# Issuing 48 weight loads from GpSimd's software queue instead of SyncE

## The chip, the core and the metric

The kernel runs on one core of a Trainium2 chip. The core has a matrix engine (TensorE, PE in the rows), VectorE (DVE), ScalarE (ACT), GpSimd (POOL) and SyncE (SP). SyncE computes nothing here: it issues transfers, which 16 DMA engines then carry out. The metric is the device time of one execution in microseconds, the median of several runs.

## What is computed

Two layers follow each other. The first is attention through a packed query, and a three-way max of matrix products; the second sends each of 4608 tokens to one of eight experts.

```python
p_packed = sm_attn(p, k, v)
out = sm_attn(q, p_packed, p_packed)          # 8 batches, 8 heads, 576 tokens, head size 64
h = np.maximum(np.maximum(x @ w1, x @ w2), x @ w3)     # 512 -> 768
x = (h @ w_out)                                        # 768 -> 512
logits = x @ w_gate
e_idx = np.argmax(logits, axis=1)
...
h = np.maximum(x[mask] @ w1[e], 0.0)          # the token's expert, 512 -> 1024 -> 512
ye = h @ w2[e]
out[mask] = gate_w[mask, None] * eom[mask, e, None] * ye
```

## The kernel before

**Stages.** The first stage takes the eight batches one after the other: attention, then the products `mm1` (L1023, its operand `G` made at L996), then rows of the first layer's output, `mm2` (L1061), which end in `yrow` in device memory. The second stage goes over blocks of 128 tokens that share an expert: `hidden` (L1307, or L1317 and L1319) and `outer` (L1365), with the expert's weights in one of two buffers, `wbuf`.

**Numbers in two halves.** Products are in 16 bits, with each operand split into a high and a low half. A split is two steps: `scaled` (L197 on ScalarE, L204 on GpSimd, L206 or L208 on VectorE) makes the high half, and `less` (L215 or L217) the low half. Which engine takes a split is open where several are allowed.

**The preparation.** The experts' weights must be split too. As soon as the first 18 of 36 row tiles are known, the kernel counts which experts are used most (`ranking`, ending in `xe`, L410), and splits the weights of the first three experts while attention goes on. `expert_of` reads an expert's number from `xe` into a register (L529). `prep` does one of 48 pieces: a load of 128 x 512 floats (256 KB) into one of four buffers `pl` (L546), the high half (`scaled`) and the low half (`less`) into one of three buffers `po`, and a store of 256 KB to the scratch `wscr` (L553). The slot pools are `rb` (four `pl`) and `rd` (three `po`); a load may not go out before the `less` that read its buffer last has ended, and a split may not begin before the store of its `po` buffer has landed. Weights of other experts are prepared in the second stage (L1384, L1399), which the change doesn't touch.

**What sets the order.** The order of every engine's instructions is written down by a planner, `Flow`. Each step has a cost per engine that may take it, a rank and a list of steps to wait for; the planner always takes the step that can start first by its own count of time, on the engine where it ends first, and the recorded order of each engine is fixed by that. Where the planner sees TensorE pause for longer than a set limit, it puts in small products on constants (`fill`, L253), whose results nobody uses. So a changed cost of one step can move everything planned after it, on all engines. Engines run their instructions strictly in order, and SyncE issues its transfers strictly in order. The program is planned in two goes; the preparation lies in the first of them (`F.run()`, L1235).

Of the kernel before, what the change touches and what calls it, by code (L numbers as in the profile page):

```python
# [18 lines left out]
SP = mybir.EngineType.SP  # L19
# [5 lines left out]
E = 8  # L25
# [25 lines left out]
class Flow:  # L51
# [18 lines left out]
    def add(self, cost, fn, after=(), rank=0, take=(), give=(), move=0.0, behind=None):  # L70

        x = types.SimpleNamespace(cost=cost, fn=fn, rank=rank, take=take, give=give, move=move, n=self.count, end=None,
                                  ready={}, by=None, wait=0, then=[], next=[])
        self.count += 1
        for y in after:
            if y is None:
                continue
            if y.end is None:
                y.then.append(x)
                x.wait += 1  # L80
            else:
                x.ready[y.by] = max(x.ready.get(y.by, 0.0), y.end)
        if behind is not None and behind.end is None:
            behind.next.append(x)
            x.wait += 1
        if not x.wait:
            self.todo.append(x)
        return x
# [70 lines left out]
def body(ctx: ExitStack, tc, q, k, v, p, w1, w2, w3, wo, wg, wog, mw1, mw2, out):  # L159
    nc = tc.nc  # L160
    w1, w2, w3, wo = (x.bitcast(I32) for x in (w1, w2, w3, wo))
    act, dve, pool, pe, sp = nc.scalar, nc.vector, nc.gpsimd, nc.tensor, nc.sync
# [19 lines left out]
    xe = const.tile([1, E], I32, name="xe")  # L182
# [7 lines left out]
    engines = dict(act=act, dve=dve, pool=pool)  # L190
    F = Flow(dict(m=3, s=2, v=1, ra=2, rt=2, rc=2, mt=1, rb=4, rd=3, w=2, wx=3, kst=1, qst=1, v16=1, pT=1, PT=1, x32=4,
                  A16=2, pp16=2, plain=1, gp=4, t0=2, t1=2, hT0=1, hT1=1, row=2))
    add = F.add
# [5 lines left out]
    def scaled(e, o, i, scale=1.0):  # L199

        if e == "act":
            act_copy(o, i, scale)
        elif e == "pool":
            pool.tensor_scalar(out=o, in0=i, scalar1=scale, scalar2=1.0, op0=ALU.mult, op1=ALU.mult)  # L204
        elif isinstance(scale, float) and scale == 1.0:
            dve.tensor_copy(out=o, in_=i)  # L206
        else:
            dve.tensor_scalar(out=o, in0=i, scalar1=scale, scalar2=None, op0=ALU.mult)  # L208

    def less(e, o, i, hi, scale=1.0):  # L210

        if e == "pool" or isinstance(scale, float) and scale == 1.0:
            if not (isinstance(scale, float) and scale == 1.0):
                scaled(e, i, i, scale)
            engines[e].tensor_tensor(out=o, in0=i, in1=hi, op=ALU.subtract)  # L215
        else:
            dve.scalar_tensor_tensor(out=o, in0=i, scalar=scale, in1=hi, op0=ALU.mult, op1=ALU.subtract)  # L217

    def costs(n, **kw):

        c = dict(act=0.09 + n * 0.834e-3, dve=0.07 + n * 1.042e-3, pool=n * 2.175e-3, both=0.02 + n * 3.28e-3, quick=0.02 + n * 1.11e-3,
                 fast=0.07 + n * 0.521e-3)
        return {dict(fast="dve", both="pool", quick="pool").get(e, e): c[e] * m for e, m in kw.items()}
# [12 lines left out]
    def placed(slot, pool, shape, dt, name):  # L236
        return Lazy(lambda tag: pool.tile(shape, dt, tag=tag, name=name, bufs=1), slot)
# [38 lines left out]
    step, rank, of = [[]], [0], {}  # L276
# [138 lines left out]
    with ExitStack() as ph1:  # L415
# [108 lines left out]
        pld, pstart, stored = [], [], {}  # L524

        def expert_of(r):

            def f(e):
                of[r] = nc.values_load(xe[0:1, r:r + 1], engines=[SP], min_val=0, max_val=E - 1)  # L529
            pstart[:] = [add(dict(sp=0.5), f, after=pstart, rank=-600)]  # L530

        def prep(n, rank=1000):
            e, u = divmod(n, 16)
            t = placed("rb", rb, [128, 512], F32, "pl")
            o = placed("rd", rd, [128, 2, 512], F16, "po")
            if u < 8:
                kt, hf = divmod(u, 2)
                src = lambda: mw1[bass.ds(of[e], 1), kt * 128:(kt + 1) * 128, hf * 512:(hf + 1) * 512].rearrange("a r f -> (a r) f")
                sc = 128.0
                dst = wscr[e, :, kt * 2048:(kt + 1) * 2048].rearrange("r (l f) -> r l f", l=2)[:, :, hf * 512:(hf + 1) * 512]  # L540
            else:
                ft = u - 8
                src = lambda: mw2[bass.ds(of[e], 1), ft * 128:(ft + 1) * 128, :].rearrange("a r f -> (a r) f")
                sc = 256.0
                dst = wscr[e, :, 8192 + ft * 1024:8192 + (ft + 1) * 1024].rearrange("r (l f) -> r l f", l=2)
            ld = add(dict(sp=0.5), lambda e: sp.dma_start(out=t()[:], in_=src()), rank=rank, take=(t,), move=0.73, after=pstart,  # L546
                     behind=pld[-1] if pld else None)
            pld.append(ld)
            h = add(costs(512, act=1, fast=1, quick=1), lambda e: scaled(e, o()[:, 0], t()[:], sc), after=[ld], rank=rank, take=(o,))
            l = add(costs(512, both=1, dve=1), lambda e: less(e, o()[:, 1], t()[:], o()[:, 0], sc), after=[h], rank=rank,  # L550
                    give=(t,))
            stored.setdefault(e, []).append(
                add(dict(sp=0.5), lambda e: sp.dma_start(out=dst, in_=o()[:]), after=[l], rank=rank - 1, give=(o,), move=0.73))  # L553
# [638 lines left out]
        for r in range(NP1):  # L1192
            expert_of(r)
        p0, p1 = plan_r[3] + T_["p0"], plan_r[B - 1]
        for n in range(NU):
            prep(n, p0 + (p1 - p0) * n * T_["prep"] / NU + V("pr", n // 8))
# [457 lines left out]
```

## Time and profile before

| | |
|---|---|
| median of 3 runs | 1003.0 us (998.7 to 1004.31) |
| the profiled execution | 998.91 us, of which the profile's span is 997.2 us |
| TensorE busy | 910.6 us, 91% of the span |
| VectorE, ScalarE, GpSimd busy | 683.1, 434.9, 382.5 us |
| mean granted clock of TensorE | 0.971 of full speed |
| loads and stores of the preparation | 48 and 48, of 256 KB each |

The span begins at 0 and stretches are given in us from there. An engine's busy time doesn't count the time in which it waits; the idle time before an instruction is put down to what ended it. Instructions that SyncE spends on issuing transfers are not in its busy time, but stand in the trace with start and length.

### The profile page before, as it was taken

What the parts mean: (1) busy time and instruction counts of PE and PEld (TensorE: products, weight loads), DVE (VectorE), ACT (ScalarE), POOL (GpSimd) and SP (SyncE); (2) the same over time, 40 slices, a digit from 0 to 9 for tenths busy, and PEclk for the clock granted to TensorE, in tenths of its full rate; (3) what the DMA queues carried; (4) which work ended last, traced back from release to release, by engine and by line L of the source; (5) the groups of instructions that cost most, each with busy time, mean ns of one, the idle gap of its engine ahead of it and who ended that gap; (6) DMA issues with size and microseconds to landing.
All of it is one profiled execution on the core that took longest, in us unless ns stands there. A gap on an engine that the chain in (4) does not pass through costs nothing. (4 is left out here: it accounts for less than half of the span.)

```text
span 997.2 us, 24407 instructions
## 1 busy us (share of the span) xinstructions
PE 910.6 (91%) x9124; PEld 672.0 (67%) x9124; DVE 683.1 (69%) x1642; ACT 434.9 (44%) x898; POOL 382.5 (38%) x494
## 2 busy tenths in 40 slices
PE   8779988969899987878799998999999999999995
PEld 6547665757676765656577786776776766767663
DVE  3998687547749479588884569588786555555551
ACT  4534544446647354243333213364564433434431
POOL 0523363647766566277533323123222221211101
PEclk9989889989999998999999999999999999999999
DMA  9965478485865769979704177523322892334930
GB/s 269 307 198 140 108 203 207 105 207 118 181 170 108 206 199 245 263 218 282 213 1 167 48 206 259 134 66 98 66 76 86 259 237 65 87 76 149 319 50 29
DMA packets 219324, 160.23 MB, mean 161 GB/s; under 512 B 155903, under 2 KB 195839, under 8 KB 216128
## 3 DMA queue, kind: packets, MB, share of 16 engines
q1 hardware_dynamic: 213280, 139.17, 52.4%
q0 software_dynamic: 5920, 19.44, 6.3%
q8 instruction: 73, 1.20, 0.5%
q14 instruction: 51, 0.42, 0.1%
HBM read 240.33 MB, written 52.99 MB: 294 GB/s over the span
## 5 line engine op out<-in xcount | busy, mean ns | idle before, releaser
L1023 PEld LDWEIGHTS <-G 128*128 128x128 f16 x1728 | 172.5, 100 | 80.8 <-issue 18.3
L1023 PE MATMUL psm<-A,G 128*128 128x288 f16 x1152 | 166.5, 295 | 25.7 <-DVE G L217 21.0
L1365 PE MATMUL pso<-wbuf,h 128*128 128x512 f16 x816 | 181.8, 379 | 1.1 <-ACTq L1620 1.1
L1061 PE MATMUL pss<-wo,hT 128*128 128x264 f16 x1296 | 152.2, 281 | 5.4 <-DVE T L959 3.8
L1365 PEld LDWEIGHTS <-h 128*128 128x128 f16 x888 | 85.3, 98 | 97.7 <-issue 1.9
L1061 PEld LDWEIGHTS <-hT 128*128 128x128 f16 x1296 | 128.5, 100 | 27.8 <-issue 6.8
L1375 POOL DMA_INDIRECT out<-o,sidx x33 | 39.9, 1208 | 259.6 <-ACT o L1370 242.6
L1317 PE MATMUL psh<-xT,wbuf 128*128 128x256 f16 x736 | 110.4, 273 | 0.0
L215 POOL TENSOR_TENSOR hT<-t,hT 128x288 f16<-128x288 f32 x84 | 66.7, 795 | 107.4 <-ACT hT L197 67.8
L1023 PE MATMUL pss<-A,G 128*128 128x288 f16 x576 | 89.4, 293 | 0.7 <-ACT e L806 0.7
L1307 PEld LDWEIGHTS <-wbuf 128*128 128x128 f16 x1344 | 77.0, 98 | 3.9 <-DMA wbuf<-wscr 1.0
L1317 PEld LDWEIGHTS <-wbuf 128*128 128x128 f16 x736 | 65.3, 98 | 9.6
L1319 PE MATMUL psh<-xT,wbuf 128*128 128x128 f16 x736 | 71.0, 219 | 0.0
L1032 DVE SCALAR_TENSOR_TENSOR t<-psm,t 128x288 f32<-128x288 f32 x96 | 43.4, 452 | 34.0 <-PE psm L1023 26.1
L197 ACT ACTIVATE t<-psm 128x288 f32<-128x288 f32 x96 | 38.8, 405 | 61.4 <-PE psm L1023 59.3
L1282 ACT ACTIVATE xs<-g,brs 128x512 f16<-128x512 f32 x37 | 26.8, 724 | 78.0 <-DVE brs L1278 76.1
L1319 PEld LDWEIGHTS <-wbuf 128*128 128x128 f16 x736 | 56.6, 98 | 4.1
L217 DVE SCALAR_TENSOR_TENSOR G<-psm,G 128x384 f16<-128x384 f32 x96 | 49.8, 546 | 11.0 <-ACT G L197 10.4
L197 ACT ACTIVATE G<-psm 128x384 f16<-128x384 f32 x96 | 43.1, 487 | 31.4 <-PE psm L996 20.9
L1326 DVE TENSOR_TENSOR hs<-psh,hs 128x512 f32<-128x512 f32 x46 | 31.8, 691 | 35.0 <-ACT hs L197 33.9
L1307 PE MATMUL psh<-xT,wbuf 128*128 128x128 f16 x960 | 55.2, 219 | 0.0
L996 PE MATMUL psm<-wst,pp 128*32 128x384 f16 x672 | 37.4, 335 | 18.7 <-DVE G L217 14.3
(295 smaller groups left out, 1531.9 us busy)
## 6 DMA issues: line engine op xcount, KB each, us to landing
wbuf<-wscr SPq DMA_DIRECT2D x148, 1024.0 KB
pt<-in_moe_w SPq DMA_DIRECT2D x40, 512.0 KB
wscr<-po SPq DMA_DIRECT2D x40, 512.0 KB
pl<-in_moe_w SPq DMA_DIRECT2D x48, 256.0 KB
wscr<-po SPq DMA_DIRECT2D x48, 256.0 KB
ld<-in_k SPq DMA_DIRECT2D x14, 512.0 KB
ld<-in_q SPq DMA_DIRECT2D x14, 512.0 KB
ld<-in_v SPq DMA_DIRECT2D x12, 512.0 KB
```

What stands on the lines that cost most here:

```text
L197: act.activation(out=o, in_=i, func=AF.Copy, scale=scale)
L215: engines[e].tensor_tensor(out=o, in0=i, in1=hi, op=ALU.subtract)
L217: dve.scalar_tensor_tensor(out=o, in0=i, scalar=scale, in1=hi, op0=ALU.mult, op1=ALU.subtract)
L996: pe.matmul(o, lhsT=a.stat(h, l), rhs=wst[:, ft, :, h, :], start=(l == 0), stop=(l == 1), tile_position=(0, hh * 32))
L1023: pe.matmul(ps()[:, 0:288], lhsT=a.G[ft]()[:, g, lg, w * 128:(w + 1) * 128], rhs=a.A16()[:, g, la, c * 288:(c + 1) * 288], start=(n == 0), ...
L1032: e0 = add(costs(288, dve=1), lambda e, src=src, o=o: dve.scalar_tensor_tensor(out=o()[:], in0=src(), scalar=sc, in1=t0()[:], op0=ALU.mult ...
L1061: pe.matmul(view()[:, nh, 0:OG0], lhsT=hT()[:, ft, lh, c0:c0 + 128], rhs=wo16()[:, ft, lw, nh, :], start=(i == 0 and ft == 0), stop=(i == ...
L1307: pe.matmul(ps[:, f4 * 128:(f4 + 1) * 128], lhsT=w1v[:, kt, lw, cols], rhs=xT[:, lx, kt, :], start=(n + kt == 0), stop=(n == 2 and kt == 3))
L1317: pe.matmul(o.rearrange("r (l t) -> r l t", l=2), lhsT=w1v[:, kt, 0, cols], rhs=xT[:, :, kt, :], start=(kt == 0), stop=False)
L1319: pe.matmul(o[:, 0:128], lhsT=w1v[:, kt, 1, cols], rhs=xT[:, 0, kt, :], start=False, stop=(kt == 3))
L1365: pe.matmul(po, lhsT=h2[:, lh, ft, :], rhs=w2v[:, ft, lw, :], start=(n == 0), stop=(n == 23))
L1375: pool.indirect_dma_start(out=out, out_offset=bass.IndirectOffsetOnAxis(ap=idx, axis=0), in_=o[:], in_offset=None, bounds_check=NTOK - 1, ...
```

## The change

Two costs and two engines are exchanged: the three register reads and the 48 loads of `prep` go to GpSimd, the load with a planned cost of 1.0 instead of 0.5. What is loaded, into which buffers and after which steps stays the same. The stores stay on SyncE.

```diff
@@ -526,8 +526,8 @@
         def expert_of(r):
 
             def f(e):
-                of[r] = nc.values_load(xe[0:1, r:r + 1], engines=[SP], min_val=0, max_val=E - 1)
-            pstart[:] = [add(dict(sp=0.5), f, after=pstart, rank=-600)]
+                of[r] = nc.values_load(xe[0:1, r:r + 1], engines=[mybir.EngineType.Pool], min_val=0, max_val=E - 1)
+            pstart[:] = [add(dict(pool=0.5), f, after=pstart, rank=-600)]
 
         def prep(n, rank=1000):
             e, u = divmod(n, 16)
@@ -543,7 +543,7 @@
...
-            ld = add(dict(sp=0.5), lambda e: sp.dma_start(out=t()[:], in_=src()), rank=rank, take=(t,), move=0.73, after=pstart,
+            ld = add(dict(pool=1.0), lambda e: pool.dma_start(out=t()[:], in_=src()), rank=rank, take=(t,), move=0.73, after=pstart,
                      behind=pld[-1] if pld else None)
```

On GpSimd, this is what stood where the preparation begins (`hT` is the low half of an `mm1` result, `pl` a loaded buffer, `po` a split one):

```order
 L215 TENSOR_TENSOR hT<-t_5203,hT 128x288
-L215 TENSOR_TENSOR hT<-t_5238,hT 128x288
-L215 TENSOR_TENSOR hT<-t_5301,hT 128x288
-L204 TENSOR_SCALAR po<-pl 128x512
-L215 TENSOR_TENSOR hT<-t_5333,hT 128x288
-L204 TENSOR_SCALAR pl<-pl 128x512
-L215 TENSOR_TENSOR po<-pl,po 128x512
-L215 TENSOR_TENSOR hT<-t_5384,hT 128x288
-L903 COPY FC<-bt 64x1
-L903 COPY FC<-bt 128x1 x4
```

And this is what stands some rows behind that place now, after the three register reads and the first four loads (the number tells one buffer's use from the next):

```order
L204 TENSOR_SCALAR pl_5306<-pl_5306 128x512
L215 TENSOR_TENSOR po_5363<-pl_5306,po_5363 128x512
L204 TENSOR_SCALAR po_5433<-pl_5338 128x512
L546 ISA
L546 DMA pl_5447<-in_moe2_w1 128x512
L546 ISA
L546 DMA pl_5455<-in_moe2_w1 128x512
L546 ISA
L546 DMA pl_5480<-in_moe2_w1 128x512
L204 TENSOR_SCALAR pl_5350<-pl_5350 128x512
L215 TENSOR_TENSOR po_5487<-pl_5350,po_5487 128x512
L204 TENSOR_SCALAR po_5530<-pl_5447 128x512
```

The loads now stand between GpSimd's splits, so that each split behind a load waits until that load can go out, and four low halves `hT` of `mm1` have left this place.

On VectorE, at the same place of the program, the piece of the difference right behind `xe` shows where they went (`t` is the input of an `hT` half):

```order
 L410 TENSOR_SCALAR xe<-fcum 1x8
+L215 TENSOR_TENSOR hT<-t_5238,hT 128x288
 L1032 SCALAR_TENSOR_TENSOR t_5276<-psm,t_5276 128x288
-L1032 SCALAR_TENSOR_TENSOR t_5301<-pss,t_5276 128x288
-L1032 SCALAR_TENSOR_TENSOR t_5320<-psm,t_5320 128x288
...
+L215 TENSOR_TENSOR hT<-t_5329,hT 128x288
+L1032 SCALAR_TENSOR_TENSOR t_5348<-psm,t_5348 128x288
+L1032 SCALAR_TENSOR_TENSOR t_5374<-pss,t_5348 128x288
+L217 SCALAR_TENSOR_TENSOR po<-pl,po 128x512
```

VectorE takes those halves now. Over the whole program the planner's counts move as follows. GpSimd loses 12 high halves `po` (31 to 19), 6 low halves `hT` (84 to 78), 4 pairs of steps on `v` (43 to 39), one pair on `vt`, 2 low halves `tm` (13 to 11) and one step on `T`; it gains the 48 loads, 2 small copies to `LG`, one step each on `e` and `ph`, and one low half `A`. VectorE gains 6 high halves `po`, 6 low halves `hT`, 4 low halves on `v` and one on `vt`, 2 low halves `tm`, one step on `T` and a cast to `A`; it loses 4 casts to `hT`, one low half `A` and two steps on `ph`. ScalarE gains 6 high halves `po` and 4 casts to `hT`. On TensorE the fill products rise from 226 to 281 (L253); all else is the same work in another order.

## Rows read from the trace of the kernel before

**Rows 1.** The page's busy times and slices of the span.

```profile
PE 910.6 (91%) x9124; PEld 672.0 (67%) x9124; DVE 683.1 (69%) x1642; ACT 434.9 (44%) x898; POOL 382.5 (38%) x494
PE   8779988969899987878799998999999999999995
DMA  9965478485865769979704177523322892334930
```

**Rows 2.** Stretches: busy us and instructions per engine, PE clock, DMA share, GB/s.

```profile
353.40:494.90 141.50, 116.06 (x1200) 87.93 (x1198) 110.62 (x201) 60.59 (x125) 91.93 (x121) 0.95 0.89 245
500.00:550.00 50.00, 48.78 (x505) 37.51 (x503) 31.62 (x83) 18.97 (x44) 17.75 (x27) 1.00 0.25 97
700.00:750.00 50.00, 50.00 (x543) 36.24 (x541) 40.78 (x93) 29.64 (x50) 14.04 (x10) 1.00 0.34 76
```

**Rows 3.** Waits of PE from 353.4 to 494.9 (total us, times, longest).

```profile
PE psm L1023 <- DVE G L217: 6.9, 5, 1.7
PE psm L996 <- DVE G L217: 6.1, 3, 5.1
PE pss L1061 <- DVE T L959: 3.8, 1, 3.8
```

**Rows 4.** SyncE's own waits at L546 in the same stretch, the three largest.

```profile
SPq L546 <- DVE t L1032: 12.5, 7, 2.6
SPq L546 <- DVE po L217: 10.4, 9, 2.6
SPq L546 <- POOL po L215: 4.6, 3, 3.1
```

**Rows 5.** The loads on SyncE: ns min/median/max, first and last start.

```profile
L546 SPq DMA_DIRECT2D pl<-in_moe_w x48: 332/344/1769, 353.5 to 486.1; - x48
```

**Rows 6.** Transfers that GpSimd issues, in the second stage (same columns).

```profile
L1265 POOL DMA_INDIRECT g<-yrow,gidx x37: 996/1042/1602, 572.4 to 933.6; - x37
L1375 POOL DMA_INDIRECT out<-o,gidx x4: 1028/1440/2479, 612.7 to 651.1; - x4
```

**Rows 7.** GpSimd's groups from 353.4 to 494.9: count, busy us, mean ns, idle before.

```profile
L204 POOL TENSOR_SCALAR po<-pl 128x512 f16<-128x512 f32 x31 | 21.1, 680 | 31.3 <-DMA wscr<-po 24.8 <-DMA pl<-in_moe_w 5.0 <-issue 1.3
L215 POOL TENSOR_TENSOR hT<-t,hT 128x288 f16<-128x288 f32 x20 | 17.4, 870 | 7.1 <-DVE hT L206 3.9 <-ACT hT L197 3.2
L215 POOL TENSOR_TENSOR v<-ld,v 128x256 f16<-128x256 f32 x8 | 6.8, 844 | 0.7
L215 POOL TENSOR_TENSOR tm<-ld,tm 128x1024 f16<-128x1024 f32 x2 | 4.7, 2369 | 0.0
L204 POOL TENSOR_SCALAR ld<-ld 128x256 f32<-128x256 f32 x8 | 4.1, 513 | 0.0
L215 POOL TENSOR_TENSOR A<-U,A 128x576 f16<-128x576 f32 x1 | 1.8, 1793 | 0.0
```

**Rows 8.** VectorE's groups in the same stretch.

```profile
L217 DVE SCALAR_TENSOR_TENSOR po<-pl,po 128x512 f16<-128x512 f32 x37 | 35.7, 968 | 15.6 <-POOL po L204 11.5 <-ACT po L197 3.8
L206 DVE CAST hT<-t 128x288 f16<-128x288 f32 x9 | 3.7, 414 | 0.3
L215 DVE TENSOR_TENSOR hT<-t,hT 128x288 f16<-128x288 f32 x5 | 3.0, 601 | 0.2
L215 DVE TENSOR_TENSOR tm<-ld,tm 128x1024 f16<-128x1024 f32 x2 | 2.9, 1446 | 0.0
L208 DVE TENSOR_SCALAR po<-pl 128x512 f16<-128x512 f32 x1 | 0.4, 427 | 1.0 <-DMA wscr<-po 1.0
```

**Rows 9.** The same low half over the whole trace, min/median/max; one on `v`.

```profile
L217 DVE SCALAR_TENSOR_TENSOR po<-pl,po x37: 674/721/2614, 356.9 to 493.0; 128x512 f16<-128x512 f32 x37
L217 DVE SCALAR_TENSOR_TENSOR v<-ld,v x5: 410/425/542, 189.4 to 326.1; 128x256 f16<-128x256 f32 x5
```

**Rows 10.** SyncE in order of time from 494: start us, us, what it issues.

```profile
493.76 0.89 SPq L553 DMA_DIRECT2D wscr<-po  x2
526.08 12.51 SPq L1080 DMA_DIRECT2D yrow<-row  x4
539.65 2.10 SPq L1260 DMA_DIRECT2D wbuf<-wscr  x4
```

**Rows 11.** The fill products around the stretch, min/median/max.

```profile
L253 PE MATMUL psv<-ones x24: 216/219/288, 385.0 to 508.7; 128*128 128x128 f16 x24
```

## Prediction

> **What bounds the kernel now.** I read the page's busy times first: TensorE is busy for 91% of the span, so only a stage in which it is not full can give or take much [rows 1]. The slices show where that is: in the last two fifths TensorE is at 9 nearly throughout, in the first half it swings between 7 and 9. Then I cut out the stretch in which the preparation runs, from the first load's issue (353.4) to its last store (494.9). There TensorE is busy for 116.1 of 141.5 us, idle for 25.4; just behind it, from 500 to 550, it is busy for 48.8 of 50, and in the second stage for all of 50 [rows 2]. So the change is worth what it does to those 25.4 us.
>
> What TensorE waits for in that stretch is mostly VectorE: 13.0 us for the low halves of `G`, which give its PSUM banks back, and 3.8 for a transpose of scores [rows 3]. VectorE is busy for 110.6 us of 141.5 (78%), GpSimd for 91.9 (65%), ScalarE for 60.6 [rows 2]. The DMA engines are in use for 0.89 of it.
>
> How late the preparation itself may be: its last store is issued at 494, the first reader, the load of `wbuf`, at 539.7 [rows 10]. That is 45 us of room, so the 48 loads don't set the end by being late. They set it by what they hold up on the engine that issues them, and by what the planner moves away from that engine.
>
> **What comes off SyncE.** 48 issues of 0.344 us [rows 5] are 16.5 us. The queue also stood still before loads: the three rows shown are 27.5 us, and four further ones of 0.7, 0.6, 0.3 and 0.2 make it 29.3 [rows 4]. These are waits for a buffer `pl` to be free again (the `less` of an earlier piece), or for an earlier transfer. Behind them stood stores, transposes and loads of attention. What is gained is bounded by what TensorE waits for: its largest waits name VectorE and none names a transfer [rows 3]. I take 0 for the gain, with 9 us as its far end (the second rival).
>
> **What comes onto GpSimd.** The trace has no plain load issued by GpSimd. From below it is bounded by SyncE's issue, 0.344 us [rows 5], from above by the slowest of its scatters in this program, 2.479, with 1.440 as that group's median [rows 6]. The nearest row is the gather: also 128 rows of about 2 KB, also issued by GpSimd, 1.042 us in the median [rows 6]. I take that: 48 x 1.042 = 50.0 us. The ends are 48 x 0.344 = 16.5 and 48 x 1.440 = 69.1. The three register reads are left at nothing: right behind them stand the first four loads, whose data the next split waits for anyway.
>
> **What the planner takes off GpSimd.** By the counts in the section on the change and the means of [rows 7]: 12 high halves `po` at 0.680 (8.2), 6 `hT` at 0.870 (5.2), 4 pairs on `v` at 0.513 + 0.844 (5.4), 2 `tm` at 2.369 (4.7); for the pair on `vt` and the step on `T` I take 3 together, the size of the larger rows here. That is 26.5. It adds one `A` at 1.793, and for two `LG`, one `e` and one `ph` I take another 3.5, so 5.3 come back. Net, 21.2 us less.
>
> GpSimd's busy time in the stretch becomes 91.9 + 50.0 - 21.2 = 120.7 us. The waits for a free `pl` come with the loads: a load on GpSimd that has to wait for VectorE's `less` holds up the split behind it, and the `hT` and attention halves behind that. Taking all 29.3 us over gives 150.0 us in a stretch of 141.5: **8.5 us too much**. This counts no wait for stores, of which GpSimd now has 24.8 us [rows 7]; I take these as the cover in which loads can go out. If that cover is gone, up to 24.8 more would be due, which is the upper bound of this term; if the loads cost 0.344, the sum is 33.5 us lower and nothing is due; if 1.440, it is 19.1 higher, which by the sum below is 1030.6.
>
> **What comes onto VectorE.** 6 `po` at 0.427, 6 `hT` at 0.601, 2 `tm` at 1.446 [rows 8], 4 `v` at 0.425 [rows 9], and about 1 each for the steps on `vt` and `T`: 2.6 + 3.6 + 2.9 + 1.7 + 2 = 12.8. Off it go 4 casts at 0.414 (1.7) and about 2.5 for `ph` and `A` together with the cast gained: 8.6 us net, 110.6 to 119.2. One thing works against it. The low half `po` took 0.968 us in the mean here [rows 8], but 0.674 at its shortest [rows 9]: over 37 of them that is 10.9 us of stretching beside other work. GpSimd's work other than loads falls from 91.9 to 70.7 us; if the stretching falls in proportion, 0.23 x 10.9 = 2.5 us are given back, and VectorE ends at about 117, 6 us more than before. The Trainium skill, SBUF — State Buffer, "Who interferes with whom", says that a VectorE instruction with two SBUF inputs contends with a GpSimd instruction that reads SBUF, and not with one that only writes it; by that, a load in place of a split would do VectorE no harm, and 6 us is the figure, where without it the sum would be the full 8.6. Since TensorE waits for VectorE by name in this stretch [rows 3], 6 us there is worth at most 6 us. It lies beside GpSimd's 8.5 us, not behind it: both stretch the same 141.5 us. I take the larger, 8.5.
>
> **The fill.** 55 more fill products at 0.219 us [rows 11] are 12.0 us at most if TensorE would otherwise have worked, and nothing where it waits anyway. The planner put them where it saw pauses; I take 0, and the upper end keeps them.
>
> **The sum.** 998.9 us, the profiled execution's time (997.2 span and 1.7 around it), + 8.5 = 1007.4. That execution is 4.1 us under the median of 1003.0, so for a median I forecast 1003.0 + 8.5 = **1011.5 us**.
>
> **Rivals.**
>
> The extra lies in idle time (no change). GpSimd idles for 49.6 us of the stretch now. If its new waits for `pl` fall together with those for stores, which stem from the same chain, 120.7 us fits into 141.5, and the moves between engines give or take a few: 1003, from 999 to 1007. For it speaks the room of 45 us [rows 10]; against it, that GpSimd would have to be busy for 85% in strict order, beside a VectorE at 83%.
>
> SyncE's freedom pays (faster). Stores would leave at once instead of behind loads. 24.8 us of GpSimd's idle time was for stores of `po` [rows 7], and VectorE's `po` halves idled 11.5 us behind GpSimd's [rows 8]; if both shrink, `G` is done sooner and TensorE's 25.4 idle us shrink by the 13.0 that name `G` less the 4 that a fuller VectorE costs: 9 us, 994. It decides if a load holds GpSimd for less than about 0.87 us: there the sum above is 141.5. The Trainium skill, DMA: Bandwidth & Descriptors, "Issuing engines are not separate DMA queues", speaks against this: all queues end on the same 16 DMA engines, and issuing from several saves only the issuer's time. By that rule the gain could be no more than SyncE's 16.5 us, which no row shows TensorE waiting for; the DMA share of 0.89 [rows 2] agrees that the transfers themselves find little room.
>
> VectorE holds up the loads' making (much slower). The price: if each of the 48 loads meets one VectorE cast of 0.414 us [rows 8], that is 20 us more on GpSimd, 28.5 in all: 1031. For it, the gathers reach 1.602 over a median of 1.042 [rows 6], 0.56 us; against it, 9 casts and a scaling fill only some 4 us of the stretch. The Trainium skill, SBUF — State Buffer, "SBUF: two separate sides", names such a mechanism: GpSimd can't write a transfer's descriptors while VectorE runs a copy or cast in a mode that uses both ports. No row here has a GpSimd transfer beside such a cast.
>
> **How the numbers follow.** Chances: forecast 0.52, no change 0.23, faster 0.17, held up by VectorE 0.08. A measurement of this kernel tells about 0.5% (5 us) from nothing. Faster by over 0.5% takes the faster rival and a little of the second's lower edge: 0.19. Same takes most of the no-change rival and a little of the forecast's lower edge: 0.25. Slower: 0.56. The range reaches from the middle of the faster rival, 995, up to 1028: the forecast with half of the 24.8 us of lost cover (1024) and a third of the fill (4); it leaves out half of the faster rival and the last one, some 17 in 100. Of the forecast alone the range is 1005 to 1028.
>
> **What would show it.** In the changed profile, the loads on GpSimd should take about 1.04 us each; GpSimd should be busy for about 120 us between the first load and the last store; waits of GpSimd at L546 for VectorE's `po` should add up to over 20 us; that stretch should be some 8 us longer, and TensorE's extra idle time should lie in it, with VectorE named. From 500 on nothing but the fill should differ. I am wrong if a load costs GpSimd much less than 0.87 us, if its waits merge, or if the new order of attention on TensorE matters more than the load on GpSimd, which no row of before can show.

## The result, and the profile after

After: 1012.74 us in the median of 8 runs (1004.82 to 1018.85), before 1000.12 us of 8 (998.45 to 1004.31): a ratio of 1.0121, 95% interval 1.0093 to 1.0150. Forecast were 1011.5 us and slower. Measured once more, in a later series of 12 runs, the same kernel gave 1.0054 (1.0026 to 1.0082). Both say slower; between them the size is 4 to 13 us, and the intervals don't overlap.

The profiled execution took 1009.87 us, with a span of 1008.3, 11.1 us more than before's. Its page, busy times, slices, granted clock and the two queues that carry the loads:

```profile
PE   913.0 (91%) x9179; PEld 673.1 (67%) x9179; DVE 688.2 (68%) x1656; ACT 437.0 (43%) x906; POOL 383.6 (38%) x516
...
PE   8779977968989978789799998999999999999997
...
PEclk9989989989999998799799999999999999999999
...
q1 hardware_dynamic: 206368, 126.58, 47.0%
q0 software_dynamic: 9760, 32.03, 11.1%
```

GpSimd's total is 383.6 us where it was 382.5 [rows 1]: the loads have come, and the planner has taken as much work away. The software queue now carries 32 MB, where it carried 19.4 before.

The stretch from the first load's preparation to the last weight store, and one in the second stage (columns as in [rows 2]):

```profile
352.70:506.60 153.90, 123.57 (x1244) 91.64 (x1242) 117.05 (x220) 67.00 (x140) 94.72 (x142) 0.90 0.86 226
...
700.00:750.00 50.00, 50.00 (x576) 36.80 (x575) 39.37 (x103) 28.26 (x49) 11.89 (x9) 1.00 0.29 80
```

The stretch is 153.9 us long, 12.4 more than before. GpSimd is busy for 94.7 of it, 62%, nowhere near full. TensorE's idle time is 30.3 us (25.4 before), and its granted clock fell from 0.95 to 0.90. The second stage is as full as it was.

The loads on GpSimd: duration in ns min/median/max, then what GpSimd stood still for just before a load (us, times). The last row is the register reads, in the same columns as the first.

```profile
L546 POOL DMA_DIRECT2D pl<-in_moe_w x48: 536/554/783, 353.4 to 485.9; - x48
...
  DVE po L217: 19.5, 18
  DVE hT L215: 4.1, 1
...
L529 POOLq TENSOR_LOAD <-xe x3: 291/297/510, 350.6 to 352.0; - x3
```

A load holds GpSimd for 0.554 us, not for the 1.042 of the gather [rows 6]. The waits for a free `pl` did come along: 19.5 us, where SyncE had 29.3 in all [rows 4]. The 4.1 us are no such wait, whatever the row names: they stand before the very first load, and the wait for `xe` and the three register reads lie in them.

GpSimd's groups in that stretch (as [rows 7]) show what went:

```profile
L204 POOL TENSOR_SCALAR po<-pl 128x512 f16<-128x512 f32 x19 | 13.9, 735 | 7.0 <-DMA pl<-in_moe_w 3.7 <-DMA wscr<-po 3.1
L215 POOL TENSOR_TENSOR po<-pl,po 128x512 f16<-128x512 f32 x11 | 13.8, 1250 | 0.9
L215 POOL TENSOR_TENSOR hT<-t,hT 128x288 f16<-128x288 f32 x15 | 12.6, 840 | 7.4 <-ACT hT L197 5.6 <-DVE hT L206 1.6
```

The 24.8 us that it had waited for stores before a high half are 3.1 now. It waits for buffers of loads in their place. VectorE, which has taken over some of those high halves, waits for stores now: 10.3 us before seven of them, where it had 1.0 before one [rows 8]; in the kernel below that has the same order with SyncE issuing it is 7.7. Its low halves wait less for GpSimd than before, 3.7 us instead of 11.5 [rows 8]:

```profile
L217 DVE SCALAR_TENSOR_TENSOR po<-pl,po 128x512 f16<-128x512 f32 x37 | 32.7, 884 | 11.0 <-ACT po L197 7.0 <-POOL po L204 3.7
L208 DVE TENSOR_SCALAR po<-pl 128x512 f16<-128x512 f32 x7 | 3.0, 421 | 10.3 <-DMA wscr<-po 10.3
```

TensorE's waits in the stretch (as [rows 3]):

```profile
PE psm L1023 <- ACT t L197: 9.8, 4, 5.1
PE pss L1023 <- ACT row L1072: 4.7, 1, 4.7
PE pss L769 <- DVE t L1032: 3.5, 2, 2.2
PE pss L1061 <- DVE row L1074: 2.7, 1, 2.7
PE psm L996 <- DVE G L217: 2.6, 4, 1.3
```

They no longer name `G` first, but ScalarE's evacuations `t` and `row`. The longest, in order of time (start us, us, what, and in brackets the idle time before it and what ended it):

```profile
409.94 5.87 SPq L622 DMA_TRANSPOSE kst<-tm  x1
...
415.90 0.53 SPq L1080 DMA_DIRECT2D yrow<-row  x1
416.53 0.38 SPq L553 DMA_DIRECT2D wscr<-po  x1
417.00 1.03 SPq L1080 DMA_DIRECT2D yrow<-row  x1
...
423.17 0.70 ACT L1072 ACTIVATE row<-pss,FC 128x528 f32<-128x528 f32 x1 [8.02 <-DMA yrow<-row]
...
424.22 1.60 PE L1023 MATMUL psm<-A,G 128*128 128x288 f16 x6 [5.10 <-ACT t L197]
424.45 0.43 DVE L208 TENSOR_SCALAR po<-pl 128x512 f16<-128x512 f32 x1 [7.29 <-DMA wscr<-po]
```

SyncE's row stores stand behind a transpose; ScalarE wants a `row` buffer and waits 8.02 us; what is behind it in its order, the next `t`, would have given TensorE its bank. TensorE stops for 5.1 us, and VectorE for 7.3. Of ScalarE's 8.02 us, 5.1 lie behind the store's issue, until it has landed. The last two rows of this section are that pause and the slice after it. In the latter (424.5 to 430) TensorE is busy throughout, at a granted clock of 0.68, so for part of it at the lower of its two levels (1.2 of 2.4 GHz):

```profile
419.00:424.50 5.50, 0.40 (x3) 0.19 (x2) 0.05 (x1) 1.30 (x3) 0.19 (x1) 0.70 0.71 268
424.50:430.00 5.50, 5.50 (x33) 3.71 (x32) 5.27 (x12) 1.37 (x3) 2.59 (x4) 0.68 0.84 284
```

To compare kernels I use one measure: from the ranking product (L400) to the first product of the second stage (first L1307). Before it is 243.3 us, after 259.4, so +16.1; ahead of it 0.7 is gained, and behind it 4.3, which make the 11.1.

### The profile page after: what moved, and what is told of

It reads as the page before. It is cut to its first block, busy times and chain, and to the rows that moved or that the text cites. A ratio compares the mean times of both kernels' runs of the same rounds, so it can differ in the third digit from the quotient of the medians.

```text
span 1008.3 us, 24545 instructions
## 1 busy us (share of the span) xinstructions
PE 913.0 (91%) x9179; PEld 673.1 (67%) x9179; DVE 688.2 (68%) x1656; ACT 437.0 (43%) x906; POOL 383.6 (38%) x516
## 3 DMA queue, kind: packets, MB, share of 16 engines
q0 software_dynamic: 9760, 32.03, 11.1%
q8 instruction: 74, 1.21, 0.5%
## 5 line engine op out<-in xcount | busy, mean ns | idle before, releaser
L1023 PE MATMUL psm<-A,G 128*128 128x288 f16 x1152 | 169.6, 298 | 30.0 <-DVE G L217 16.3
L215 POOL TENSOR_TENSOR hT<-t,hT 128x288 f16<-128x288 f32 x78 | 61.6, 790 | 99.5 <-ACT hT L197 62.5
L1307 PEld LDWEIGHTS <-wbuf 128*128 128x128 f16 x1344 | 76.6, 98 | 3.6 <-DMA wbuf<-wscr 0.7
L1326 DVE TENSOR_TENSOR hs<-psh,hs 128x512 f32<-128x512 f32 x46 | 31.8, 691 | 35.2 <-ACT hs L197 34.0
L1307 PE MATMUL psh<-xT,wbuf 128*128 128x128 f16 x960 | 55.2, 219 | 0.0
L1335 DVE SCALAR_TENSOR_TENSOR h<-hs,h 128x512 f16<-128x512 f32 x46 | 31.8, 692 | 32.0 <-ACT h L1332 32.0
```

The lines of the kernel that those rows point to most:

```text
L1023: pe.matmul(ps()[:, 0:288], lhsT=a.G[ft]()[:, g, lg, w * 128:(w + 1) * 128], rhs=a.A16()[:, g, la, c * 288:(c + 1) * 288], start=(n == 0), ...
L1307: pe.matmul(ps[:, f4 * 128:(f4 + 1) * 128], lhsT=w1v[:, kt, lw, cols], rhs=xT[:, lx, kt, :], start=(n + kt == 0), stop=(n == 2 and kt == 3))
L1326: dve.tensor_tensor(out=hv, in0=parts[:, :, 0, :], in1=hv, op=ALU.add)
```

## Experiments

All ratios are to before, on the same chip as the run itself. The order is the sequence of instructions that the planner gives each engine; where two kernels are said to have the same order, TensorE's, VectorE's and ScalarE's sequences are equal row for row, but for the loads themselves.

**Who issues, and which order.** Theory A: what GpSimd is held for costs. Theory B: the planner's new order costs. The first kernel keeps before's planned costs and lets GpSimd issue; the second keeps after's and lets SyncE issue:

```
(e1) add(dict(sp=0.5), lambda e: pool.dma_start(out=t()[:], in_=src()), ...)
(e2) add(dict(pool=1.0), lambda e: sp.dma_start(out=t()[:], in_=src()), ...)
```

> The loads and the register reads are issued by GpSimd, but the planner still counts them as SyncE's at 0.5: TensorE, VectorE, ScalarE keep the order of before, only GpSimd's and SyncE's queues change. If the loss comes from GpSimd's holding the loads and their waits (A), this is slower by 8 to 12 us, ratio 1.008 to 1.012. If it comes from the new order that the planner made (B), this is within 4 us of before, 0.996 to 1.004, and 0.554 us a load is hidden in GpSimd's idle time.

> The planner counts the loads as GpSimd's at 1.0, as in the changed kernel, but SyncE issues them: TensorE, VectorE and ScalarE have the changed kernel's order, the loads are back on SyncE. By A this is within 4 us of before, 0.996 to 1.004. By B it is as slow as the changed kernel, 1.009 to 1.015; above that if SyncE, filled again, holds up attention's transfers in an order that was not made for it.

Measured: GpSimd in the old order 1.0055 (1.0030 to 1.0080); SyncE in the new order 1.0006 (0.9979 to 1.0033). The windows from L400 to L1307, of before, of the first and of the second:

```profile
347.80:591.10 243.30, 214.49 (x2161) 165.40 (x2161) 178.06 (x372) 91.61 (x193) 123.33 (x166) 0.97 0.64 181
```

```profile
348.30:601.50 253.20, 220.50 (x2161) 168.96 (x2161) 181.24 (x372) 91.84 (x193) 148.34 (x214) 0.93 0.60 174
```

```profile
346.70:591.60 244.90, 218.53 (x2217) 168.55 (x2217) 177.87 (x386) 95.73 (x201) 101.43 (x140) 0.97 0.62 179
```

The old order with GpSimd issuing loses 9.9 us there, of which 3.9 are more idle time of TensorE (28.8 to 32.7) and 6.0 longer work with the same 2161 products, at a granted clock of 0.93 instead of 0.97. The new order with SyncE issuing loses 1.6. B falls: this order alone costs nothing that can be measured. A holds in kind, not in size: GpSimd issuing in the old order costs about 5 us, where A expected 8 to 12. From the second kernel to after, the order being the same, 14.5 us are lost between the two traces; the second kernel's was the fastest of its 12 runs, 4 us under their median, so not all of that is the issuer. TensorE's waits in the second kernel, over the same part of the program, show where after's grew:

```profile
PE psm L1023 <- ACT t L197: 5.0, 2, 3.7
PE pss L1023 <- ACT row L1072: 2.6, 1, 2.6
```

These 7.6 us for ScalarE's `t` and `row` are 14.5 in after, which is 6.9 of the 8.8 us by which TensorE's idle time there grows.

**Another planned cost.** The load planned at 0.55 us, on GpSimd (`dict(pool=0.55)`) and, as a control, on SyncE (`dict(sp=0.55)`); each gives yet another order.

> As the changed kernel, but with a planned cost of 0.55 for a load on GpSimd, what the profile after shows (0.554). By A about the same as the changed kernel, 1.008 to 1.013, since GpSimd's true work stays. By B it is a third order, with fewer planned pauses (275 fill products against 281, 226 before): nothing fixes its sign, and it should lie between 0.998 and 1.012.

> Loads on SyncE as before, with a planned cost of 0.55 instead of 0.5, which changes no work and no engine of any transfer, but lets the planner make another order (248 fill products). By A 0.997 to 1.003. By B another order costs by itself: 1.003 to 1.015, with new pauses of several us of TensorE in the preparation's stretch.

1.0031 (1.0007 to 1.0056) and 1.0035 (1.0009 to 1.0060). The control, which changes no engine, is as slow as the other: an order of its own can cost 0.35%. Both lie in B's range, the first of them well under A's 1.008 to 1.013. So these two tell nothing of the issuer, and the 0.3% between plans is the grain below which one kernel of this planner can't be compared with another. Planning with the true cost was not better than before either.

**GpSimd held, without the software queue.** SyncE issues; at each load's place GpSimd either clears the load's own buffer (it stands still for the buffer, and is then held as long as by a load), or clears a small tile of its own four times (held, but waits for nothing).

```
(e7, e9)   pool.memset(t()[:, 0:512], 0.0); sp.dma_start(out=t()[:], in_=src())
(e8, e10)  4 x pool.memset(scrap[:], 0.0);  sp.dma_start(out=t()[:], in_=src())
```

In the old order:

> The order of before on every engine; SyncE issues the 48 loads as before, but GpSimd clears the load's own buffer first (one memset of 128x512, estimated at 0.5 us between the 0.288 us of 128x224 and the 0.951 us of 128x1024). So GpSimd stands still for each free buffer and is held about 0.5 us per load, as when it issues the load itself, but nothing goes through the software queue. Theory W (GpSimd's standing still in order, with the time it is held): ratio to before 1.003 to 1.008, near the 1.0055 of the run in which GpSimd issues in the old order, with some 15 to 25 us of waits of that memset. Theory Q (what the software queue does to the transfers): 0.998 to 1.002.

> The order of before; SyncE issues the loads; at each load's place GpSimd clears a small tile of its own four times (4 x about 0.14 us), which waits for nothing. So it is held as long as by a load, but never stands still for a buffer. Theory W, if the standing still is what costs: 0.999 to 1.002. Theory T (the 27 us of GpSimd's time alone delay its halves of the weights): 1.003 to 1.007. Theory Q: 0.998 to 1.002.

In the new order:

> The order of after, loads issued by SyncE (as in the run of the new plan alone, 1.0006), and GpSimd clears the load's own buffer first. Theory W: 1.008 to 1.014, as after itself (1.012). Theory Q: 0.998 to 1.003.

> The order of after, loads issued by SyncE, GpSimd clears a small tile of its own four times at each load's place and waits for nothing there. Theory W with standing still as the cost: 0.999 to 1.004. Theory T: 1.005 to 1.010. Theory Q: 0.998 to 1.003.

Measured, old order: held with the wait 1.0064 (1.0038 to 1.0089), held without it 1.0042 (1.0019 to 1.0066). New order: 1.0057 (1.0040 to 1.0075) and 1.0015 (0.9990 to 1.0040). GpSimd's groups for the four, in that order (count, busy us, mean ns, idle before):

```profile
L547 POOL MEMSET pl<- 128x512 f32 x48 | 24.9, 524 | 16.8 <-DVE po L217 16.4
```

```profile
L549 POOL MEMSET scrap<- 128x64 f32 x192 | 29.9, 155 | 8.6
```

```profile
L547 POOL MEMSET pl<- 128x512 f32 x48 | 24.8, 529 | 16.7 <-DVE po L217 16.3
```

```profile
L549 POOL MEMSET scrap<- 128x64 f32 x192 | 29.6, 154 | 9.4
```

The doses are those of the loads: some 25 to 30 us of time, 16 us of waits. Theory Q (the software queue's transfers cause all of it) falls, since 0.6% is lost in either order without that queue. Between waiting and being held the two orders differ. In the old one the time alone already costs 0.42%, and the wait adds nothing that the intervals can tell. In the new one the time alone isn't told from nothing, and time and wait together cost 0.57%, between what W (1.008 to 1.014) and Q (0.998 to 1.003) expected.

The stand-in with the wait does more than it is meant to, though. The load that SyncE issues must wait until GpSimd has cleared its buffer, and SyncE, in order, stands still with it; in after SyncE has none of these loads. SyncE's waits of this kind in the old and in the new order (us, times, longest):

```profile
SPq L548 <- POOL pl L547: 31.9, 21, 3.0
```

```profile
SPq L548 <- POOL pl L547: 10.9, 10, 2.8
```

So the 0.57% isn't the price of GpSimd's own waits alone; how much of it is SyncE's was not tested. The small tile that waits for nothing doesn't tie the loads to GpSimd, and the 0.42% in the old order is the cleanest figure here. Being held never filled GpSimd: over the 250.7 us from L400 to L1307 it is busy for 145.8 in the old order with time alone.

Who feels it is seen on VectorE, in the group of low halves `po`, which wait for GpSimd's high halves. In [rows 8] that wait is 11.5 us. With GpSimd issuing in the old order (e1), with time alone there (e8), and in the new order with SyncE issuing (e2), around the same stretch:

```profile
L217 DVE SCALAR_TENSOR_TENSOR po<-pl,po 128x512 f16<-128x512 f32 x37 | 37.7, 1019 | 24.2 <-POOL po L204 21.1 <-ACT po L197 2.7
```

```profile
L218 DVE SCALAR_TENSOR_TENSOR po<-pl,po 128x512 f16<-128x512 f32 x37 | 35.6, 965 | 25.8 <-POOL po L205 18.9 <-ACT po L198 6.8
```

```profile
L217 DVE SCALAR_TENSOR_TENSOR po<-pl,po 128x512 f16<-128x512 f32 x37 | 29.6, 801 | 10.6 <-POOL po L204 5.2 <-ACT po L197 4.8
```

In the old order 31 high halves are GpSimd's, and its held time goes straight into VectorE's wait: 11.5 to 18.9 us by the time alone. The new order leaves GpSimd 19 of them, and the wait is 5.2 us to begin with. That is a likely reason why the time alone costs little there. In after itself the wait is 3.7 us, so this chain is not what after loses by.

**Fewer waits, another issuer, and after again.** From after: each load is issued two GpSimd instructions later; from the second kernel: ScalarE issues; and after itself beside them.

```
(e11) late.append([2, lambda: pool.dma_start(out=t()[:], in_=src())])
(e12) act.dma_start(out=t()[:], in_=src())
```

> After itself, the order of the other engines unchanged, but on GpSimd each load is issued two of its other instructions later than the plan says (at the latest just before the load's first reader). The time per load is as in after (0.55 us); what should go is most of the 19.5 us for which GpSimd stood still for a buffer that VectorE had not freed. Theory W (in the new order standing still is what costs: 1.0057 with it against 1.0015 without it, SyncE issuing): 1.006 to 1.010, and the waits for VectorE's `po` before the load under 8 us. Theory T (the time alone) and theory Q (the software queue's transfers, which would land later still): 1.010 to 1.018.

> The order of after, but ScalarE issues the 48 loads through its hardware queue: neither SyncE nor GpSimd is held by them, ScalarE is (SyncE's median of 0.34 us per issue would make 16 us, beside 67 us of work in that stretch, and waits for free buffers come on top). Theory S (that SyncE runs ahead without the loads is the other half of what after loses): 1.004 to 1.012, with the row stores awaited by ScalarE as in after (14.7 us). Theory Q (the software queue is): 0.998 to 1.004, with those waits near the 10.4 us that they are where SyncE issues.

> After itself, on the chip of these runs, to compare with the others. All theories: 1.009 to 1.015.

Measured 1.0113 (1.0072 to 1.0154), 1.0090 (1.0056 to 1.0123) and 1.0054 (1.0026 to 1.0082). The last is below what was expected of it. GpSimd's waits for `po` before the later loads:

```profile
  DVE po L237: 10.1, 10
```

TensorE's waits with the later loads, then in after on this chip:

```profile
PE psm L1043 <- ACT t L217: 15.6, 6, 8.8
...
PE pss L1043 <- ACT row L1092: 3.1, 1, 3.1
```

```profile
PE psm L1023 <- ACT t L197: 8.9, 4, 3.1
...
PE pss L1023 <- ACT row L1072: 4.0, 1, 4.0
```

The waits before the loads halved, short of the 8 us that was expected, and the kernel got no faster: by the medians, 1011.43 and 1004.25 us, it is the slower of the two on this chip, with TensorE waiting 15.6 us for ScalarE's `t`. By their ratios T and Q expected this one. Theory W, as a claim that the standing still is the cost to be removed, finds no support; the interval still reaches into its range (1.006 to 1.010). With ScalarE issuing, neither GpSimd nor the software queue is touched, and 0.9% is lost as well. That is in the range of theory S, that SyncE without the loads does harm, though ScalarE's waits for row stores are 9.6 us there, as where SyncE issues, and not the 14.7 that S wanted. ScalarE's own delay explains the loss as well: TensorE waits for that engine's `t` for 13.5 us, 7.5 at the longest. S got a test of its own.

**The row stores off SyncE.** After, with all 56 row stores on ScalarE's queue.

```
- sp.dma_start(out=yrow[...], in_=rf()[r0:r1])
+ act.dma_start(out=yrow[...], in_=rf()[r0:r1])
```

> After, but ScalarE issues the 56 row stores through its hardware queue, so that they no longer stand in SyncE's order behind weight stores that wait for a late `po`. Theory S (TensorE's pauses in the new order come of row stores stuck on SyncE): ScalarE's waits for a row store in the weights' stretch fall from 14.7 and 11.3 us (the two traces of after) to under 5, TensorE's waits for ScalarE's `t` and `row` from 14.5 and 12.9 us to under 9, and the ratio is 1.000 to 1.005. Theory T (GpSimd's time makes the halves of the weights late, whatever SyncE does): the waits for the row store may fall, but the ratio stays at 1.005 to 1.013.

Measured: 1.0159 (1.0132 to 1.0187). ScalarE's waits for a row store, 14.7 us in after, are gone from the stretch. TensorE's are not:

```profile
PE psm L1023 <- ACT t L197: 12.8, 5, 4.7
PE psm L1023 <- DVE t L1032: 9.4, 1, 9.4
```

So with the row store of 423 us out of the way TensorE stands still for 9.4 us behind VectorE: that store was one of several late things there. The kernel is slower even than theory T allowed. S finds no support in this form, but the test is not clean: it puts 56 issues, of 0.45 us in the median, in front of ScalarE's own work, and 48 loads on ScalarE cost 0.9% by themselves. After was not run on this chip.

## Why the prediction was right, and where not

**The number: near by luck in part.** 1011.5 us stood on a median of 1003.0 for before, from three runs, where eight gave 1000.12. As a change, 8.5 us were forecast; 12.6 were measured, and 4.2 in the later series.

**What bounds it, and where the loss lies: right.** Of the 16.1 us up to the second stage 12.4 lie in the stretch, and the products of the second stage are unchanged.

**What comes off SyncE is worth nothing: right as far as the runs go.** No kernel in which SyncE was free of the loads beat before. The Trainium skill, DMA: Bandwidth & Descriptors, "Issuing engines are not separate DMA queues", gave SyncE's time as the most that could be won; no run here won any of it.

**The load's cost: mis-sized.** 0.554 us in place of 1.042, so 48 of them are 27 us, not 50; the waits for buffers are 19.5 us, not 29.3. The register reads, left at nothing, took up 4.1 us of GpSimd's time with the wait for `xe`. GpSimd's busy time in the stretch is 94.7 us, not 120.7.

**The step that failed is the criterion behind it:** that GpSimd loses time once its work and waits exceed the 141.5 us, with 0.87 us per load as the point below which SyncE's freedom pays. By that rule the measured load would have made the kernel faster, or left it alone: 94.7 us of work and 23.6 of waits fit into 141.5. It is slower, with GpSimd busy for 62%. The forecast of +8.5 us came out near the result because a load too dear met a criterion too lenient. In its place the runs showed order and lateness. GpSimd issuing costs 0.55% in the old order, and some 0.6 us put 48 times in front of GpSimd's work, without any wait, already costs 0.42% there, on an engine that is idle for much of the stretch: VectorE's low halves wait longer for GpSimd's high ones. In the new order that wait is short, and the time alone cost nothing that can be told; what grows from the second kernel to after is TensorE's wait for ScalarE's `t` and `row`, 7.6 to 14.5 us (12.9 in after's second trace). That these come late because VectorE, SyncE and ScalarE work in order behind a load on GpSimd is read from the waits and was not isolated.

**Part of the price may be the clock.** From the second kernel to after (same order, same products) TensorE's idle time grows by 8.8 us (26.4 to 35.2) and its busy time by 5.7, while the granted clock falls from 0.97 to 0.93:

```profile
347.10:606.50 259.40, 224.19 (x2216) 171.01 (x2216) 182.43 (x386) 95.01 (x201) 125.52 (x188) 0.93 0.63 170
```

The prediction had no such term: in its stretch, too, only 4.9 of the 12.4 us are more idle time. That the lower clock costs the 5.7 us is not shown. Ahead of L400 the same 3221 products took 304.2 us before and 297.2 after, at 0.95 and 0.97, and the time up to there differs by only 0.7 us, so longer work can come out of idle time.

**VectorE: near the size forecast, not decisive.** 117.05 us in the stretch, forecast 117, but in a stretch that is 12.4 us longer and has 19 more of its instructions; over the whole span VectorE gained 5.1 us (683.1 to 688.2). That a load in place of a split does VectorE no harm is not borne out: in the same order the 37 low halves took 801 ns in the mean with SyncE issuing and 884 in after; in the old order 968 and, with GpSimd issuing, 1019. TensorE's extra waits name ScalarE.

**The fill: right.** The second kernel has the 55 products too and stands at 1.0006.

**VectorE holding up the loads' making: not seen.** A load takes 536 ns at the least and 783 at the most. The Trainium skill, SBUF — State Buffer, "SBUF: two separate sides", speaks of such a stop; in the issue, as the trace shows it, it could be no more than 0.25 us, and that in the first load alone; the others stay under 0.6 us, and the median is 18 ns above the shortest.

**What stays open.** The size. After lost 1.21% in one series and 0.54% in the other, with the same program. Its stand-in without the software queue lost 0.57% in the new order, without the 3.8 us at the end of the run that the software queue gives back (below). So the loads may cost something beyond GpSimd's time and waits: from L400 to L1307 after took 259.4 and 254.6 us in its two traces, the stand-in 252.7. After's two traces differ by more than the smaller of these gaps, and the old order doesn't settle it: 253.2 with GpSimd issuing against 249.0, but the latter trace was the fastest of its six runs, 5.7 us under their median. Whether there is such a rest, and whether it is the other queue's transfers, a SyncE that runs ahead, or the register reads, which the stand-ins left on SyncE, the runs didn't separate; a kernel that holds SyncE alone, with GpSimd issuing, was not tried. Nor was one with more `pl` buffers.

## What to carry to other kernels

A DMA issue moved to an engine that computes is not priced by that engine's idle share: it stands in order ahead of that engine's next result, and so does its wait for a buffer. Ask which results stand behind it and who waits for those, and test the cost with a stand-in instruction of the same length, one that ties no other engine to it, before blaming the queue. Where a planner reorders everything, measure the new order with the old issuer first, and an arbitrary third order as a control.

## What was not expected of the hardware

A plain load of 128 rows of 2 KB held GpSimd for 0.554 us through the software queue, 0.344 us was its issue on SyncE [rows 5].

Kernels that send these loads through the software queue end sooner after their last scatter. That scatter's last start, in after and in before, whose spans are 1008.3 and 997.2 us:

```profile
L1375 POOL DMA_INDIRECT out<-o,sidx x33: 977/999/1861, 677.2 to 1004.1; - x33
```

```profile
L1375 POOL DMA_INDIRECT out<-o,sidx x33: 979/1004/1860, 662.0 to 989.3; - x33
```

That is 4.2 us to the end against 7.9. It is 4.1 or 4.2 in all six traces with the loads on the software queue, and 7.9 or 8.0 in all eight others, that with ScalarE's queue among them. No engine computes in those last microseconds, so their cause is open. It is a gain of 3.8 us, of the 4.3 that the second stage gave back: ahead of that stage after had lost 15.4 us in the profiled execution, where the span shows 11.1.
